# Attention and a gated feed-forward layer on one core: in the first four pairs of heads, the row sums of the softmax move from ScalarE's exponentials to matmuls with ones

## The chip, the cores and the metric

One core of one Trainium2 chip. The metric is the time of one execution in device microseconds; a kernel is run several times and the median is given. All data is float32 in memory. Times inside the program come from one profiled execution.

## What is computed

```python
scores = q @ k.T / sqrt(64)                 # 8 batches, 8 heads, 576 positions, 64 columns
scores = where(row // 64 >= col // 64, scores, -1e9)
attn = exp(scores - max(scores, axis=-1))
attn = attn / (sum(attn, axis=-1) + 1e-9)
x = (attn @ v) as [4608, 512]
h = x @ w_in                                # 512 -> 2048
out = (h / (1 + exp(-1.702 * h))) @ w_out   # 2048 -> 512
```

## The kernel before, in words

**Pairs of heads.** Two heads share the 128 partitions of q and k, so there are 32 pairs (n from 0 to 31), four to a batch. The 576 query rows of a head are cut into five chunks: chunk 0 has 64 rows, chunks 1 to 4 have 128. With the block mask, chunk i sees 64*(2i+1) columns: 64, 192, 320, 448 and 576.

**A pair's way.** `prep` turns q and k with two VectorE transposes (L297), so that their columns lie on the partitions. `score` multiplies them into PSUM banks; chunk 4 is written in two parts, 256 and 320 columns. `weigh` reads a bank on VectorE (L351: add the mask, scale by -0.125, and keep each row's minimum, which is the maximum with its sign turned) and writes the distances to the tile `turned`; then ScalarE takes the exponential in place with the minimum as bias and sums the row in the same instruction (L358). `normalise` adds 1e-9 to the sum and takes the reciprocal on VectorE (L368, L371) and multiplies the chunk by it on GpSimd (L376). `flip` (used for pairs 0 to 7) turns the chunk on TensorE by matmuls with the identity (L102) into a bank, up to four 128x128 squares in each, and ScalarE copies that bank to the second half of `turned` (L411, L424). `av` multiplies the turned weights with v into two banks, o (512 query columns, chunks 1 to 4) and o0 (64, chunk 0), 30 matmuls for a pair; ScalarE copies both to `xr` (L450, L451), the input of the second stage. An fp32 matmul appears as two records in the profile. Later pairs (8 to 31) turn their weights on VectorE and by DMA instead.

**The second stage.** `moe` walks over tiles of 384 of the 4608 rows. `split` cuts a tile of `xr` into a high and a low part in float32r (ScalarE L498, VectorE L82). For each of 16 units of 128 hidden columns there are 12 matmuls into one bank `hp`, a tanh on ScalarE (L562), the gate on VectorE (L563), a cast and a subtraction that split the result (L571, L82), and nine matmuls into the three `acc` banks. The first tile needs all heads of its rows, so pairs 0 to 3. The weights arrive as words of 64 bits and are turned into float32 and split, piece after piece (32 pieces): ScalarE starts a piece (L219), VectorE merges in three steps (L223, L229, L234), ScalarE casts the high part (L243), GpSimd subtracts the low one (L82). One PSUM bank serves these pieces one at a time.

**Order.** TensorE's instructions stay in program order (`mm` and `tr` say so). For the first four pairs it is: scores of chunks 1 and 0 of pair n, turning of chunks 2 and 3 of pair n-1, scores of chunks 2 and 3, turning of chunk 4 of pair n-1, scores of chunk 4, products of pair n-1 with v, turning of chunks 0 and 1 of pair n. On the other engines a scheduler fixes the order when the program is built; each engine then works through its queue in that order, and an instruction that waits holds up all that stands behind it. The PSUM banks of the attention are handed out in a ring of seven by `bank()` until the second stage begins; a bank is used again once its last reader is done. The distances have one buffer for each chunk, shared by all early pairs, and so have the turned weights.

Of the kernel before, what the change touches and what calls it, by code (L numbers as in the profile page):

```python
# [10 lines left out]
F32 = mybir.dt.float32  # L11
F32R = mybir.dt.float32r
U32 = mybir.dt.uint32
AF = mybir.ActivationFunctionType
ALU = mybir.AluOpType
# [14 lines left out]
)  # L30

START = "1+0 - B 2/3 L C - V - 4 - a - - -"
HANDOVER = "B C - 3+0/2+1 - - V - - - 4 - - L - -"
# [7 lines left out]
def attention_moe_kernel(  # L41
# [9 lines left out]
    nc = tc.nc  # L51
    B, H, S, D = q.shape
    DM, DF = w_in.shape
    P = 128
    BLK = 64
# [8 lines left out]
    HP = H // 2  # L64
    NCH = 5

    sp = ctx.enter_context(tc.tile_pool(name="sp", bufs=1))
# [6 lines left out]
    def early(n):  # L74

        return n < 2 * HP

    def phase(n):
        return 0 if n < HP else 1 if n < 2 * HP else 2
# [9 lines left out]
    def bank():  # L89
        tags = ["w0", "w1", "w2"]  # L90
        if not turns["experts"]:
            tags += ["acc0", "acc1", "acc2", "h"]
        elif turns["n"] > 2 * HP:
            tags.append("w3")
        turns["bank"] += 1
        return ps.tile([P, 512], F32, tag=tags[turns["bank"] % len(tags)], name="bank")

    def mm(**kw):
        return tc.keep_in_program_order(nc.tensor.matmul(**kw))  # L99
# [32 lines left out]
    vp = sp.tile([P, 2, NCH, D], F32, name="vp")  # L132
    nc.gpsimd.memset(vp[BLK:P, :, NCH - 1, :], 0.0)
    vx = {}

    def values(n):

        if n not in (1, 3):
            return vp
        if n not in vx:  # L140
            vx[n] = room("xl", [P, 2, NCH, D], F32, "vx")
            nc.gpsimd.memset(vx[n][BLK:P, :, NCH - 1, :], 0.0)
        return vx[n]
# [140 lines left out]
    def load_v(n):  # L284
        to = values(n)
        for hd, b, h in heads(n):
            nc.sync.dma_start(
                out=to[:, hd, 0:QC], in_=v[b, h, 0 : QC * P].rearrange("(c p) d -> p c d", p=P)
            )
            nc.sync.dma_start(out=to[0:BLK, hd, QC], in_=v[b, h, QC * P : S])  # L290
# [49 lines left out]
    def weigh(n, i, hd, lo, hi, s, e):  # L340
        mx, sm = stats[n]
        a, z = qrange(i)
        m = z - a
        w = width(i)
        if early(n):
            e = es[i]
        elif e is None:
            e = d2.tile([P, 2, w], F32, tag=f"e{i % 2}", name="e", bufs=1)
        last = i > 0 and hi == w
        mk = mask[0:m, MW - (hi - lo) : MW] if last else mask[0:m, 0 : hi - lo]  # L350
        nc.vector.tensor_tensor_reduce(  # L351
            out=e[0:m, hd, lo:hi], in0=s, in1=mk,
            op0=ALU.add, op1=ALU.min, scale=-0.125,
            scalar=3e38 if lo == 0 else mx[0:m, NCH, hd : hd + 1],
            accum_out=mx[0:m, i, hd : hd + 1] if hi == w else mx[0:m, NCH, hd : hd + 1],
        )
        if hi == w:
            nc.scalar.activation(  # L358
                out=e[0:m, hd], in_=e[0:m, hd], func=AF.Exp, scale=-1.0,
                bias=mx[0:m, i, hd : hd + 1], accum_out=sm[0:m, i, hd : hd + 1],  # L360
            )
        return e

    def normalise(n, i, e):
        _, sm = stats[n]
        m = BLK if i == 0 else P
        c = sm[0:m, i]
        nc.vector.tensor_scalar(  # L368
            out=c, in0=c, scalar1=1e-9, scalar2=2.0, op0=ALU.add, op1=ALU.mult
        )  # L370
        nc.vector.reciprocal(out=c, in_=c)  # L371
        on = SCALE_ON[phase(n)][i]
        for hd in range(2):
            x, sc = e[0:m, hd], c[:, hd : hd + 1]
            if on == "P":
                nc.gpsimd.tensor_tensor(out=x, in0=x, in1=sc.to_broadcast([m, width(i)]), op=ALU.mult)  # L376
            elif on == "D":
                nc.vector.tensor_scalar(out=x, in0=x, scalar1=sc, scalar2=None, op0=ALU.mult)  # L378
            else:
                nc.scalar.activation(out=x, in_=x, func=AF.Copy, scale=sc)  # L380
# [19 lines left out]

    def flip(n, chunks):

        for i in chunks:
            todo = [(j, hd) for j in range(i) for hd in range(2)]
            for x in range(0, len(todo), 4):
                part = todo[x : x + 4]
                bk = bank()
                for y, (j, hd) in enumerate(part):
                    tr(out=bk[:, y * P : (y + 1) * P], in_=es[i][:, hd, j * P : (j + 1) * P], identity=ident)
                s0 = SLOT[i] + part[0][0]  # L410
                nc.scalar.copy(  # L411
                    out=pw[:, :, s0 : s0 + len(part) // 2].rearrange("p b s h c -> p (s h) b c"),
                    in_=bk[:, 0 : len(part) * P].rearrange("p (x b c) -> p x b c", b=4, c=32),
                )

        bk = bank()
        todo = [(i, hd) for i in chunks for hd in range(2)]
        for y, (i, hd) in enumerate(todo):
            tr(out=bk[0:BLK, y * P : (y + 1) * P], in_=es[i][:, hd, i * P : width(i)], identity=ident)
        src = bk[0:BLK, 0 : len(todo) * P].rearrange("p (x b c) -> p x b c", b=4, c=32)  # L420
        for part in ([0], [1]) if 0 in chunks else (chunks,):
            i, x, a = part[0], 2 * chunks.index(part[0]), 2 if part[0] else 0
            s0 = 9 + max(i, 1)
            nc.scalar.copy(  # L424
                out=pw[0:BLK, a : a + 2, s0 : s0 + len(part)].rearrange("p b s h c -> p (s h) b c"),
                in_=src[:, x : x + 2 * len(part), a : a + 2],
            )

    def av(n):

        b, h = divmod(n, HP)
        before_av(n)
        o, o0 = bank(), bank()

        todo = []
        for i in range(1, NCH):
            c = (i - 1) * P
            todo += [(o, c, P, j, pw[:, :, SLOT[i] + j]) for j in range(i)]
            todo.append((o, c + BLK, BLK, i, pw[:, 2:4, 9 + i]))
        last = len(todo) - 1  # L440
        todo.append((o0, 0, BLK, 0, pw[:, 0:2, 10]))

        for x, (bk, c, nn, j, w) in enumerate(todo):
            for hd in range(2):
                mm(
                    out=bk[hd * D : hd * D + D, c : c + nn].rearrange("d (a c) -> d a c", c=32),
                    lhsT=values(n)[:, hd, j], rhs=w[:, :, hd], start=x in (0, last + 1), stop=x >= last,
                )
        c0 = (b % 2) * S
        nc.scalar.copy(out=xr[:, h, c0 : c0 + BLK], in_=o0[:, 0:BLK])  # L450
        nc.scalar.copy(out=xr[:, h, c0 + BLK : c0 + S], in_=o)  # L451
        m = follower(n)
        if m is not None:
            load_v(m)

    def follower(n):

        m = {0: 2, 1: 3, 2: 4, 3: None}.get(n, n + 1)
        return None if m is None or m >= NPAIR else m
# [205 lines left out]
```

## Time and profile before

| what | value |
|---|---|
| median of 3 runs | 1122.48 us (1120.67 to 1125.02) |
| the profiled execution | 1120.49 us, span 1118.6 us, mean TensorE clock 0.992 |
| TensorE busy | 1076.4 us, 96% of the span |
| VectorE, ScalarE, GpSimd busy | 583.0, 498.6, 406.7 us |
| first matmul of the second stage | 76.91 us |

The page has the span in 40 slices of 28 us; a digit is the busy share of a slice in tenths. A row of a timeline gives the start, the duration, the engine, the line, the operation, what it writes and reads, and in brackets how long the engine stood idle before it and what ended that. A group's row ends with its busy time, the mean of one in ns, and the idle time ahead of it. The engines are PE (TensorE), DVE (VectorE), ACT (ScalarE), POOL (GpSimd).

### The profile page before, as it was taken

What the parts mean: (1) busy time and instruction counts of PE and PEld (TensorE: products, weight loads), DVE (VectorE), ACT (ScalarE), POOL (GpSimd) and SP (SyncE); (2) the same over time, 40 slices, a digit from 0 to 9 for tenths busy, and PEclk for the clock granted to TensorE, in tenths of its full rate; (3) what the DMA queues carried; (4) which work ended last, traced back from release to release, by engine and by line L of the source; (5) the groups of instructions that cost most, each with busy time, mean ns of one, the idle gap of its engine ahead of it and who ended that gap; (6) DMA issues with size and microseconds to landing.
All of it is one profiled execution on the core that took longest, in us unless ns stands there. A gap on an engine that the chain in (4) does not pass through costs nothing. (4 is left out here: it accounts for less than half of the span.)

```text
span 1118.6 us, 19977 instructions
## 1 busy us (share of the span) xinstructions
PE 1076.4 (96%) x6960; PEld 908.7 (81%) x6960; DVE 583.0 (52%) x1856; ACT 498.6 (45%) x1321; POOL 406.7 (36%) x509
## 2 busy tenths in 40 slices
PE   5969998999999999999999999999999999999998
PEld 3757776788888888888888888888888888899997
DVE  6776885545545555654555655645545654211210
ACT  5866776434534433534443543444434444322322
POOL 4665664333333332333333333333333233122222
PEclk9979999999999999999999999999999999999999
DMA  8734532332444432343443333344342332200000
GB/s 171 205 89 153 150 73 62 84 79 57 105 86 86 103 80 64 64 98 78 98 101 74 75 93 65 70 108 85 81 107 63 71 85 58 54 29 1 29 1 29
DMA packets 219365, 91.25 MB, mean 82 GB/s; under 512 B 197760, under 2 KB 197760, under 8 KB 219264
## 3 DMA queue, kind: packets, MB, share of 16 engines
q1 hardware_dynamic: 214528, 89.38, 34.0%
q10 hardware_dynamic: 4736, 0.59, 0.3%
q8 instruction: 55, 0.90, 0.3%
q14 instruction: 46, 0.38, 0.1%
HBM read 45.09 MB, written 9.44 MB: 49 GB/s over the span
## 5 line engine op out<-in xcount | busy, mean ns | idle before, releaser
L82 POOL TENSOR_TENSOR gl<-g,gh 128x384 fp32r<-128x384 f32 x192 | 194.7, 1014 | 551.5 <-ACT gh L571 449.1
L99 PE MATMUL hp<-xh,wih 128*128 128x384 f32 x768 | 264.7, 345 | 7.9 <-DVE g L563 6.9
L563 DVE SCALAR_TENSOR_TENSOR g<-g,hp 128x384 f32<-128x384 f32 x192 | 105.9, 552 | 319.1 <-ACT g L562 317.8
L99 PE MATMUL hp<-xh,wil 128*128 128x384 f32 x768 | 258.4, 336 | 0.1
L562 ACT ACTIVATE g<-hp 128x384 f32<-128x384 f32 x192 | 94.1, 490 | 359.8 <-PE hp L99 354.8
L99 PE MATMUL hp<-xl,wih 128*128 128x384 f32 x768 | 253.9, 338 | 0.4 <-DVE xl L82 0.4
L99 PE MATMUL acc<-woh,gh 128*128 128x512 f32 x576 | 233.9, 406 | 0.0
L99 PE MATMUL acc<-wol,gh 128*128 128x512 f32 x576 | 226.9, 394 | 0.0
L99 PEld LDWEIGHTS hp<-xh,wih 128*128 128x128 f32 x768 | 144.2, 188 | 34.1 <-DVE g L563 23.1
L99 PE MATMUL acc<-woh,gl 128*128 128x512 f32 x576 | 167.9, 393 | 0.3 <-POOL gl L82 0.3
L571 ACT CAST gh<-g 128x384 fp32r<-128x384 f32 x192 | 98.4, 513 | 156.5 <-DVE g L563 156.4
L99 PEld LDWEIGHTS hp<-xh,wil 128*128 128x128 f32 x768 | 144.3, 188 | 6.5 <-POOL wil L82 0.7
L358 ACT ACTIVATE e<-e,mx 64x64 f32<-64x64 f32 (+4 forms) x240 | 132.3, 552 | 37.6 <-DVE mx L351 37.6
L376 POOL TENSOR_TENSOR e<-e,sm 64x64 f32<-64x64 f32 (+1 forms) x192 | 113.6, 612 | 95.0 <-DVE sm L371 46.5
L99 PEld LDWEIGHTS hp<-xl,wih 128*128 128x128 f32 x768 | 143.6, 188 | 1.3 <-DVE xl L82 1.3
L99 PE MATMUL bank<-qk 64*128 64x320 f32 (+4 forms) x768 | 122.5, 428 | 14.5 <-DVE qk L297 11.1
L99 PEld LDWEIGHTS acc<-woh,gh 128*128 128x128 f32 x576 | 107.9, 187 | 34.2 <-issue 10.5
L99 PEld LDWEIGHTS acc<-woh,gl 128*128 128x128 f32 x576 | 107.8, 188 | 25.9 <-POOL gl L82 1.2
L99 PEld LDWEIGHTS acc<-wol,gh 128*128 128x128 f32 x576 | 108.3, 188 | 16.7 <-POOL wol L82 0.3
L351 DVE CUSTOM_DVE_ANT_0 e<-bank,mask 64x64 f32<-64x64 f32 (+4 forms) x240 | 89.7, 417 | 56.9 <-PE bank L99 52.8
L385 DVE STREAM_TRANSPOSE turned<-e 128x384 f32<-128x384 f32 (+1 forms) x192 | 92.3, 499 | 48.8 <-POOL e L376 48.3
L99 PEld LDWEIGHTS bank<-qk 64*128 64x128 f32 x768 | 69.6, 193 | 54.2 <-issue 25.4
(50 smaller groups left out, 956.0 us busy)
## 6 DMA issues: line engine op xcount, KB each, us to landing
turned<-turned SPq DMA_DIRECT2D x192, 80.0 KB, 2.1
turned<-turned SPq DMA_DIRECT2D x96, 112.0 KB, 2.2
raw<-in_q_dram SPq DMA_DIRECT2D x128, 72.0 KB, 2.4
out_dram<-osb SPq DMA_DIRECT2D x36, 256.0 KB, 2.2
raw<-in_k_dram SPq DMA_DIRECT2D x120, 72.0 KB, 2.6
turned<-turned SPq DMA_DIRECT2D x96, 88.0 KB, 2.1
words<-in_moe_w_in_dram SPq DMA_DIRECT2D x16, 512.0 KB, 6.3
vp<-in_v_dram SPq DMA_DIRECT2D x60, 128.0 KB, 2.4
```

The costliest lines, as they stand in the source:

```text
L82: eng.tensor_tensor(out=out, in0=in0, in1=in1, op=ALU.subtract)
L99: return tc.keep_in_program_order(nc.tensor.matmul(**kw))
L351: nc.vector.tensor_tensor_reduce(out=e[0:m, hd, lo:hi], in0=s, in1=mk, op0=ALU.add, op1=ALU.min, scale=-0.125, scalar=3e38 if lo == 0 else ...
L358: nc.scalar.activation(out=e[0:m, hd], in_=e[0:m, hd], func=AF.Exp, scale=-1.0, bias=mx[0:m, i, hd : hd + 1], accum_out=sm[0:m, i, hd : hd ...
L376: nc.gpsimd.tensor_tensor(out=x, in0=x, in1=sc.to_broadcast([m, width(i)]), op=ALU.mult)
L385: nc.vector.transpose(out=tw[:, :, SLOT[i] : SLOT[i] + i, hd].rearrange("p b j c -> p j b c"), in_=e[:, hd, 0 : i * P],)
L562: nc.scalar.activation(out=g, in_=hp[:, 0:tt], func=AF.Tanh, scale=1.702)
L563: nc.vector.scalar_tensor_tensor(out=g, in0=g, scalar=1.0, in1=hp[:, 0:tt], op0=ALU.add, op1=ALU.mult)
L571: nc.scalar.copy(out=gh, in_=g)
```

## The change

For pairs 0 to 3 the rows are no longer divided by their sums before they are turned. `weigh` now subtracts the row's minimum from the distances on GpSimd, without an exponential; `normalise` does nothing. `flip` turns the distances on TensorE, and ScalarE takes the exponential where it copied a bank before. `av` takes a third bank and multiplies the turned weights with a tile of ones, in 28 matmuls for chunks 1 to 4 and two for chunk 0, which leaves the sum of each row in all 64 partitions of its head; then come the 30 products with v. VectorE adds 1e-9 and multiplies by 2, takes the reciprocal, and multiplies the output bank by it into `xr`: three operations on 128x512 and three on 128x64, where ScalarE had two copies. The constant `ones` is set once by GpSimd.

```diff
+    def raw_turned(n):
+        return n < HP
...
+    ones = sp.tile([P, D], F32, name="ones")
+    nc.gpsimd.memset(ones, 1.0)
...
-        if hi == w:
+        if hi == w and raw_turned(n):
+            nc.gpsimd.tensor_tensor(
+                out=e[0:m, hd], in0=e[0:m, hd], in1=mx[0:m, i, hd : hd + 1].to_broadcast([m, w]), op=ALU.subtract
+            )
+        elif hi == w:
             nc.scalar.activation(
                 out=e[0:m, hd], in_=e[0:m, hd], func=AF.Exp, scale=-1.0,
...
     def normalise(n, i, e):
+        if raw_turned(n):
+            return
...
+        def move(out, in_):
+            if raw_turned(n):
+                nc.scalar.activation(out=out, in_=in_, func=AF.Exp, scale=-1.0)
+            else:
+                nc.scalar.copy(out=out, in_=in_)
...
+        c0 = (b % 2) * S
+        if raw_turned(n):
+            o1 = bank()
+            todo0 = [(o0, BLK, BLK, 0, pw[:, 0:2, 10])]
+            sums = [(o1, *x[1:]) for x in todo]
+
+            for some, base in ((sums, ones), (todo0, ones), (todo, None)):
+                for x, (bk, c, nn, j, w) in enumerate(some):
+                    for hd in range(2):
+                        mm(
+                            out=bk[hd * D : hd * D + D, c : c + nn].rearrange("d (a c) -> d a c", c=32),
+                            lhsT=values(n)[:, hd, j] if base is None else base, rhs=w[:, :, hd],
+                            start=x == 0, stop=x == len(some) - 1,
+                        )
+            for hd in range(2):
+                mm(
+                    out=o0[hd * D : hd * D + D, 0:BLK].rearrange("d (a c) -> d a c", c=32),
+                    lhsT=values(n)[:, hd, 0], rhs=pw[:, 0:2, 10, hd], start=True, stop=True,
+                )
+            for a, c, r in ((o, BLK, o1[:, 0:512]), (o0, 0, o0[:, BLK : 2 * BLK])):
+                w = r.shape[1]
+                to = xr[:, h, c0 + c : c0 + c + w]
+                nc.vector.tensor_scalar(out=to, in0=r, scalar1=1e-9, scalar2=2.0, op0=ALU.add, op1=ALU.mult)
+                nc.vector.reciprocal(out=to, in_=to)
+                nc.vector.tensor_tensor(out=to, in0=a[:, 0:w], in1=to, op=ALU.mult)
+            m = follower(n)
+            if m is not None:
+                load_v(m)
+            return
```

In `flip` the two calls of `nc.scalar.copy` become calls of `move`. TensorE's order is the same but for the 30 new matmuls in each of the four pairs.

VectorE's queue between the last scores of pair 2 and the transposes that make ready pair 3 (`qk`), before:

```order
L351 ISA turned_75,mx_433<-bank_546,mask_69,mx_433 128x320
L351 ISA mx_433 128x1
L297 STREAM_TRANSPOSE qk_512<-raw_172 128x576
L368 TENSOR_SCALAR sm_434<-sm_434 128x2
L371 RECIPROCAL sm_434<-sm_434 128x2
L297 STREAM_TRANSPOSE qk_512<-raw_172 128x576
```

and the same place with the change (bank_541 and bank_542 hold pair 1's output, bank_543 its sums):

```order
L358 ISA turned_77,mx_430<-bank_527,mask_69,mx_430 128x320
L358 ISA mx_430 128x1
L304 STREAM_TRANSPOSE qk_493<-raw_158 128x576
L483 TENSOR_SCALAR xr_72<-bank_543 128x512
L484 RECIPROCAL xr_72<-xr_72 128x512
L483 TENSOR_SCALAR xr_72<-bank_542 128x64
L485 TENSOR_TENSOR xr_72<-bank_541,xr_72 128x512
L304 STREAM_TRANSPOSE qk_493<-raw_158 128x576
L484 RECIPROCAL xr_72<-xr_72 128x64
L485 TENSOR_TENSOR xr_72<-bank_542,xr_72 128x64
```

Four of the six new operations stand ahead of the second transpose.

The output of pair 2 before, on ScalarE's queue (bank_762 and bank_763 are its banks; L243 and L219 belong to the weights' pieces):

```order
L243 CAST woh_410<-wm_369 128x512
L219 ACTIVATE wm_416<-words_285 128x512
L243 CAST woh_410<-wm_430 128x512
L219 ACTIVATE wm_460<-words_414 128x512
L451 COPY xr_72<-bank_762 128x512
L450 COPY xr_72<-bank_763 128x64
L411 COPY turned_75<-bank_804 128x2x4x32
L498 CAST xh_977<-xr_72 128x384
```

and with the change, on VectorE's queue (bank_754 and bank_755 hold the output, bank_756 the sums; L230, L236 and L241 are the three merging steps, L358 on bank_849 are pair 4's first scores):

```order
L483 TENSOR_SCALAR xr_72<-bank_756 128x512
L484 RECIPROCAL xr_72<-xr_72 128x512
L304 STREAM_TRANSPOSE qk_702<-raw_286 128x576
L230 TENSOR_SCALAR wm_413<-wm_413 128x512
L236 SCALAR_TENSOR_TENSOR wm_413<-words_259,wm_413 128x512
L241 SCALAR_TENSOR_TENSOR wm_427<-words_259,wm_413 128x512
L230 TENSOR_SCALAR wm_449<-wm_449 128x512
L236 SCALAR_TENSOR_TENSOR wm_449<-words_411,wm_449 128x512
L485 TENSOR_TENSOR xr_72<-bank_754,xr_72 128x512
L241 SCALAR_TENSOR_TENSOR wm_490<-words_411,wm_449 128x512
L483 TENSOR_SCALAR xr_72<-bank_755 128x64
```

The multiplication that empties the output bank stands behind the transpose and five merging steps of two pieces.

The output of pair 3 with the change, again on VectorE (bank_966 and bank_967 hold it, bank_968 the sums; L87 makes the low part of the second stage's first tile, qk_929 is for pair 5):

```order
L483 TENSOR_SCALAR xr_72<-bank_968 128x512
L241 SCALAR_TENSOR_TENSOR wm_678<-words_498,wm_653 128x512
L484 RECIPROCAL xr_72<-xr_72 128x512
L87 TENSOR_TENSOR xl_1040<-xr_72,xh_1039 128x384 x3
L230 TENSOR_SCALAR wm_700<-wm_700 128x512
L304 STREAM_TRANSPOSE qk_929<-raw_705 128x576
L236 SCALAR_TENSOR_TENSOR wm_700<-words_651,wm_700 128x512
L485 TENSOR_TENSOR xr_72<-bank_966,xr_72 128x512
L241 SCALAR_TENSOR_TENSOR wm_731<-words_651,wm_700 128x512
L483 TENSOR_SCALAR xr_72<-bank_967 128x64
L484 RECIPROCAL xr_72<-xr_72 128x64
L485 TENSOR_TENSOR xr_72<-bank_967,xr_72 128x64
```

where before the two copies stood on ScalarE right behind pair 3's last copies out of the turned banks:

```order
L411 COPY turned_75<-bank_920 128x4x4x32
L424 COPY turned_75<-bank_926 64x2x2x32
L451 COPY xr_72<-bank_939 128x512
L450 COPY xr_72<-bank_940 128x64
L498 CAST xh_977<-xr_72 128x384
L243 CAST wih_643<-wm_674 128x512
```

The output's last step moved from ScalarE, where nothing stood between the products and the cast, to VectorE behind other work.

More of the change, by code (lines that the diff above doesn't have):

```diff
@@ L410, in flip @@
                 s0 = SLOT[i] + part[0][0]
-                nc.scalar.copy(
+                move(
                     out=pw[:, :, s0 : s0 + len(part) // 2].rearrange("p b s h c -> p (s h) b c"),
@@ L423, in flip @@
             s0 = 9 + max(i, 1)
-            nc.scalar.copy(
+            move(
                 out=pw[0:BLK, a : a + 2, s0 : s0 + len(part)].rearrange("p b s h c -> p (s h) b c"),
@@ L448, in av @@
                 )
-        c0 = (b % 2) * S
         nc.scalar.copy(out=xr[:, h, c0 : c0 + BLK], in_=o0[:, 0:BLK])
```

## The prediction

> **What bounds the kernel now.** I read the page's slices first, then the waits of TensorE in the first 77 us, then the timelines of TensorE, ScalarE and VectorE there, and last VectorE's groups by form. The page's slices (28 us each), busy tenths of TensorE and its granted clock:
>
> ```profile
> PE   5969998999999999999999999999999999999998
> PEclk9979999999999999999999999999999999999999
> ```
>
> From the fourth slice on TensorE is full, so the span is a start plus a stretch that TensorE sets. The change touches only the first four pairs, which lie in the start; what counts is when the second unit of the experts' first layer begins (81.60 in a row below), since TensorE hardly waits behind it. The waits of TensorE from 0 to 77 us (total, times, longest):
>
> ```profile
> PE bank L99 <- DVE qk L297: 11.1, 4, 7.2
> PE bank L102 <- ACT xr L450: 3.1, 1, 3.1
> PE bank L99 <- ACT turned L411: 2.3, 2, 1.6
> PE bank L102 <- POOL turned L376: 2.2, 1, 2.2
> ```
>
> Of the first row 7.2 us is the first load; the other 3.9 are waits for q and k of the next pair to be turned. TensorE's timeline of the start (start, us, engine, line, operation, count in matmul records, two for one matmul in fp32):
>
> ```profile
> 7.23 5.71 PE L99 MATMUL bank<-qk 64*128 64x192 f32 x24 [7.23 <-DVE qk L297]
> ...
> 32.15 0.76 PE L99 MATMUL bank<-qk 64*128 64x192 f32 x8 [0.58 <-DVE qk L297]
> 32.84 1.75 PE L102 MATMUL bank<-ident,turned 128*128 128x128 f32 x14
> 34.52 1.98 PE L99 MATMUL bank<-qk 64*128 64x320 f32 x8
> 36.42 1.31 PE L102 MATMUL bank<-ident,turned 128*128 128x128 f32 x10
> 37.67 1.24 PE L99 MATMUL bank<-qk 64*128 64x256 f32 x8
> 38.84 2.99 PE L99 MATMUL bank<-turned,vx 128*64 128x128 f32 x60
> 41.75 0.88 PE L102 MATMUL bank<-ident,turned 128*128 128x128 f32 x6
> 43.42 0.76 PE L99 MATMUL bank<-qk 64*128 64x192 f32 x8 [0.79 <-DVE qk L297]
> ...
> 52.38 2.98 PE L99 MATMUL bank<-turned,vp 128*64 128x128 f32 x60
> ...
> 58.69 0.76 PE L99 MATMUL bank<-qk 64*128 64x192 f32 x8 [2.52 <-DVE qk L297]
> ...
> 63.16 2.37 PE L102 MATMUL bank<-ident,turned 128*128 128x128 f32 x10 [3.12 <-ACT xr L450]
> 66.33 3.88 PE L99 MATMUL bank<-qk 64*128 64x320 f32 x8 [0.80 <-ACT turned L424]
> 70.14 2.39 PE L102 MATMUL bank<-ident,turned 128*128 128x128 f32 x10
> 72.46 3.73 PE L99 MATMUL bank<-turned,vx 128*64 128x128 f32 x60
> ...
> 81.60 0.44 PE L99 MATMUL hp<-xh,wih 128*128 128x384 f32 x1 [1.79 <-DVE g L563]
> ```
>
> Rows 32.15 to 41.75 are one pair on a TensorE that hardly waits: 0.76 + 1.75 + 1.98 + 1.31 + 1.24 = 7.04 us from its first scores to its last, 2.99 for the products with v, 0.88 to turn the next two chunks. From 63.16 on the same work takes about twice as long, 4.8 us more over four rows: the clock has dropped. Why TensorE waits at 63.16 stands on ScalarE's queue (casts and first steps of the weights' conversion, then the copies that empty the bank):
>
> ```profile
> 61.35 0.62 ACT L243 CAST woh<-wm 128x512 fp32r<-128x512 f32 x1 [2.29 <-DVE wm L234]
> 61.88 0.62 ACT L219 ACTIVATE wm<-words 128x512 f32<-128x512 f32 x1
> 62.44 0.58 ACT L451 COPY xr<-bank 128x512 f32<-128x512 f32 x1
> 62.91 0.21 ACT L450 COPY xr<-bank 128x64 f32<-128x64 f32 x1
> ```
>
> The products ended at 52.38 + 2.98 = 55.36; the copy that frees their bank stood behind two casts that wait for VectorE. So an instruction that empties a bank is priced by what is queued ahead of it.
>
> **The change, part by part.** VectorE's groups by form (count, busy, mean ns):
>
> ```profile
> L297 DVE STREAM_TRANSPOSE qk<-raw 128x576 f32<-128x576 f32 x64 | 46.7, 758 | 5.8 <-DMA raw<-in_q_dram 5.7
> L82 DVE TENSOR_TENSOR xl<-xr,xh 128x384 fp32r<-128x384 f32 x48 | 27.1, 605 | 22.5 <-ACT xh L498 22.0 <-PE bank L99 0.5
> L223 DVE TENSOR_SCALAR wm<-wm 128x512 uint32<-128x512 uint32 x32 | 22.3, 696 | 15.9 <-ACT wm L219 15.9
> L229 DVE SCALAR_TENSOR_TENSOR wm<-words,wm 128x512 uint32<-128x512 uint32 x28 | 19.3, 688 | 0.3
> L234 DVE SCALAR_TENSOR_TENSOR wm<-words,wm 128x512 uint32<-128x512 uint32 x28 | 19.0, 680 | 0.7
> L371 DVE RECIPROCAL sm<-sm 128x2 f32<-128x2 f32 x128 | 21.0, 164 | 3.7
> L351 DVE CUSTOM_DVE_ANT_0 turned<-bank,mask 128x448 f32<-128x448 f32 x16 | 9.7, 613 | 4.9 <-PE bank L99 4.9
> L351 DVE CUSTOM_DVE_ANT_0 turned<-bank,mask,mx 128x320 f32<-128x320 f32 x16 | 8.4, 537 | 0.1
> L351 DVE CUSTOM_DVE_ANT_0 turned<-bank,mask 128x320 f32<-128x320 f32 x16 | 7.5, 484 | 0.6 <-PE bank L99 0.3
> L351 DVE CUSTOM_DVE_ANT_0 turned<-bank,mask 128x256 f32<-128x256 f32 x16 | 6.5, 414 | 0.9 <-PE bank L99 0.9
> L351 DVE CUSTOM_DVE_ANT_0 turned<-bank,mask 128x192 f32<-128x192 f32 x16 | 5.1, 341 | 0.0
> L351 DVE CUSTOM_DVE_ANT_0 turned<-bank,mask 64x64 f32<-64x64 f32 x16 | 3.2, 210 | 3.8 <-PE bank L99 3.7
> ```
>
> *TensorE* gets 30 matmuls more for a pair, of the shapes of row 38.84: 2.99 us, 12.0 for four pairs, in its fixed order and so on the path. *ScalarE* loses ten exponentials, their sums and two copies for a pair, and its nine copies out of the turned banks become exponentials. I take those at the copies' price; they add nothing to the end while ScalarE has the freed time. *GpSimd* keeps ten full-size operations for a pair, a subtraction where a multiplication was, of the same sizes: nothing, but they wait for VectorE's minima alone. That takes away the 2.2 us wait for GpSimd.
>
> *VectorE* loses ten small operations and gets six with a pair's output: add and multiply on 128x512 (0.70, by row L223), a reciprocal, a multiplication with the output bank (0.69, by row L229), and the same on 64 columns (0.2, by the 64x64 row, except the reciprocal). A wide reciprocal is not in the trace. VectorE's timeline has a narrow one:
>
> ```profile
> 52.53 0.15 DVE L371 RECIPROCAL sm<-sm 128x2 f32<-128x2 f32 x1
> 52.60 0.40 DVE L351 CUSTOM_DVE_ANT_0 turned<-bank,mask 128x256 f32<-128x256 f32 x1
> ```
>
> The next instruction starts 0.07 us behind it, so an element costs at most 35 ns: 512 cost at most 18 us. At least they cost what other arithmetic of that shape does, 0.70. One row has the shape, the other the operation, and neither is near, so I take their geometric middle, 3.5 us, an estimate; for 64 columns 0.65 between 0.2 and 2.2. The Trainium skill, "VectorE: DVE Perf Modes", section "Walkthrough: the 8-slice pipeline in each mode", has the reciprocal as an iterated divide with a repeat count of 8; were that eight passes for each element, at 1.0 ns for a column (the 448 against the 320 row) it would be 4.1 us, an estimate, and the sum below some 3 us longer; no run here shows it.
>
> What lies behind these six on VectorE is what costs: the second transpose for the next pair (all of the next scores wait for it), and the release of the banks. By the queue orders shown above:
>
> 1. *To the products of pair 0.* TensorE's first scores end at 12.94. VectorE's queue then holds two transposes (1.52), the last four scores of pair 0 (1.90), eight of pair 1 (3.30) and four of six merging steps (2.76) before the bank for pair 1's last scores is free: from 12.35 to 21.9, so they end at 22.3, the last matmul being 0.4. Sums and products, 2 x 2.98: 28.2.
> 2. *Scores of pair 2.* VectorE from 21.9: 1.37 of merging, 1.90 of scores, 0.76 of transpose, 25.9; then 0.70 + 3.5 + 0.2 + 0.69 + 0.65 + 0.2 and the second transpose, 0.76: 32.6. Before 32.15: the gain is gone.
> 3. *Scores of pair 3.* 32.6 + 7.04 + 2.99 puts the sums at 42.6; 0.70 + 3.5 + 0.2 + 0.69 + 0.76: 48.5. Before 43.42, +5.1.
> 4. *Scores of pair 4.* From 48.5 VectorE has 0.85 left of pair 1, 0.42 of scores, then two pieces' merging among pair 3's scores: 2.07 + 0.68 + 0.97 + 0.61 + 0.70 + 0.61, 55.4. There the last scores of pair 3 can start; the sums of pair 2 are done at 58.9. VectorE goes on: 0.69 + 0.41 + 0.68 + 0.41 + 1.07, then 1.38 + 0.76 + 0.68 of piece 4 and a transpose, 61.5; 0.70 + 3.5 + 0.76: 66.5. Before 58.69, +7.8.
> 5. *The banks of pair 2's output.* VectorE then merges piece 5 (2.07), waits for ScalarE's cast and start of piece 6 (1.24), does two steps of it (1.38), and only then multiplies the output (0.69); a merge (0.68) and 1.5 on 64 columns follow. The banks are free at 74.1; before at 63.16, +10.9.
> 6. *To the experts.* At the low clock the rows from 63.16 to 72.46 take 9.3 again: 83.4. Sums 3.73: 87.1. VectorE: 0.70 + 0.68 + 3.5, three subtractions for the experts' first tile (1.8), 0.70 + 0.76 + 0.69, the multiplication, 0.69 + 0.68, 64 columns 1.05: 98.4. ScalarE's cast of that column block is over at 99; the seventh matmul of the first unit waits for it, where before it came right behind the products. From that matmul to 81.60 it was 3.7 us: 102.6. That is 21.0 us later; I take off 0.6 for one cast that stood before the first tanh and by the order now stands ahead of this wait, and call it 20.
>
> The profiled execution took 1120.49 us (span 1118.6), 2.0 below the median of three, 1122.48. 1120.5 + 20 = 1140.5 against the profile; as the median I say 1141.
>
> **Rivals.** *The reciprocal runs at the plain rate*, 0.7 and 0.2. Steps 2, 3 and 4 then end at 29.4, 43.8 and 58.5: pairs cost what they did, with 12 us of matmuls paid by the waits that go. Step 5 gives 65.6 and step 6 an end 9 us later: 1130. For it speaks that the narrow reciprocal is no longer than its neighbours, against it only how little a row of two elements can say.
>
> *No change.* The plain rate, and the scheduler's queue behind pair 2 is harmless since the merges ahead of the multiplication run while VectorE would idle, so that TensorE keeps its clock: 1130 less 4.8 and less part of the 3 us of ScalarE's wait: 1123. Against it speaks that each merge waits for ScalarE's cast of the piece before, on one bank.
>
> *Faster*, one mechanism: the idle time of TensorE pays for the sums. Place: its stalls from 12.9 to 77 us. Price: the waits above come to 11.5 us without the first load, the low clock costs 4.8; with the 12.0 us of new matmuls that is 4 us less, and up to 8 less if the smaller waits go too: 1116 to 1112. It decides if VectorE's output work of pairs 0 to 2 is over within 1 us of the products, so that no transpose and no bank waits for it; then a wide reciprocal may not cost over about 1 us, and merging may not stand ahead of pair 2's multiplication. In the queue's order it does stand there.
>
> That the work does not move is no rival: the order shows the new operations.
>
> **Numbers.** My case 0.56, the plain rate 0.26, no change 0.11, faster 0.07. A measurement tells 0.5%, 5.6 us, from no change. My case is slower; of the plain rate I count 0.21 as slower and 0.05 as within. So slower 0.77, same 0.16, faster 0.07. The range reaches from the lower part of the plain rate, 1124, to a reciprocal over 4 us with two or three more us of low clock, 1150.
>
> **What would show it.** Right: a wide RECIPROCAL of some us on VectorE; scores of pair 3 near 48 us and of pair 4 near 66, waiting for qk; the transposes of chunks 2 and 3 of pair 3 waiting for VectorE until over 70; the second unit of the experts near 102; unchanged group means behind it. Wrong: a wide reciprocal under 1 us; the start not longer than 82 us; exponentials out of the banks clearly above the copies' 0.58; a shift that is not in the first 110 us.

## The result, and the profile after

The changed kernel takes 1131.68 us (four runs, 1130.99 to 1133.36) where the kernel before, run beside it, takes 1123.75: a ratio of 1.0075, with a 95% interval from 1.006 to 1.0091. So it is slower by 7.9 us; forecast was 1141, in a range from 1124 to 1150. Its profiled execution took 1131.48 us (span 1129.7), 11.0 more than the profiled execution of before.

The page's slices show where: the second to the fourth read 867, where before they read 969, and behind them TensorE is as full as before.

```profile
PE   7867999999999999999999999999999999999998
PEclk9988999999999999999999999999999999999999
```

To say how late each stretch is, I compare the start of the same instruction in both traces: ScalarE's cast that begins to split the result of a unit of the experts' first layer (192 of them). Its first one, its 13th, its 16th and its last, before and then after (start, duration):

```profile
81.58 0.51 ACT L571 CAST gh<-g 128x384 fp32r<-128x384 f32 x1
166.30 0.50 ACT L571 CAST gh<-g 128x384 fp32r<-128x384 f32 x1
197.41 0.51 ACT L571 CAST gh<-g 128x384 fp32r<-128x384 f32 x1 [1.71 <-DVE g L563]
1111.61 0.51 ACT L571 CAST gh<-g 128x384 fp32r<-128x384 f32 x1 [0.62 <-DVE g L563]
```

```profile
95.22 0.50 ACT L619 CAST gh<-g 128x384 fp32r<-128x384 f32 x1
180.34 0.53 ACT L619 CAST gh<-g 128x384 fp32r<-128x384 f32 x1
207.45 0.51 ACT L619 CAST gh<-g 128x384 fp32r<-128x384 f32 x1 [1.71 <-DVE g L611]
1122.63 0.51 ACT L619 CAST gh<-g 128x384 fp32r<-128x384 f32 x1 [0.62 <-DVE g L611]
```

The shift is +13.6 us at the first unit, +14.0 at the 13th, +10.0 at the 16th, +11.0 at the last. All of the loss is made in the first 95 us; then 4 us are given back between 166 and 208 us, and 1 us is lost again behind that.

The three largest waits of TensorE from 0 to 100 us after (total, times, longest):

```profile
PE bank L104 <- DVE qk L304: 15.0, 5, 7.4
PE hp L104 <- ACT xh L546: 6.5, 1, 6.5
PE bank L107 <- DVE xr L485: 5.2, 2, 4.7
```

They are those for q and k (15.0, before 11.1), for the multiplication that empties an output bank (5.2; before 3.1, for a copy), and one of 6.5 that was 0.7 before, for the cast of pair 3's output. The waits for GpSimd have gone, as forecast. TensorE's timeline:

```profile
21.53 2.99 PE L104 MATMUL bank<-turned,ones 128*64 128x128 f32 x60
24.35 2.94 PE L104 MATMUL bank<-turned,vp 128*64 128x128 f32 x60
...
30.76 0.76 PE L104 MATMUL bank<-qk 64*128 64x192 f32 x8 [2.67 <-DVE qk L304]
...
45.50 0.76 PE L104 MATMUL bank<-qk 64*128 64x192 f32 x8 [1.90 <-DVE qk L304]
...
63.17 0.76 PE L104 MATMUL bank<-qk 64*128 64x192 f32 x8 [2.80 <-DVE qk L304]
...
68.60 1.09 PE L107 MATMUL bank<-ident,turned 128*128 128x128 f32 x4 [4.67 <-DVE xr L485]
70.19 2.37 PE L107 MATMUL bank<-ident,turned 128*128 128x128 f32 x10 [0.50 <-DVE xr L485]
72.49 2.34 PE L104 MATMUL bank<-qk 64*128 64x320 f32 x8
74.76 1.31 PE L107 MATMUL bank<-ident,turned 128*128 128x128 f32 x10
76.00 2.62 PE L104 MATMUL bank<-turned,ones 128*64 128x128 f32 x44
...
91.21 0.69 PE L104 MATMUL hp<-xh,wih 128*128 128x384 f32 x1 [6.51 <-ACT xh L546]
...
94.67 0.69 PE L104 MATMUL hp<-xh,wih 128*128 128x384 f32 x1 [1.17 <-DVE g L611]
```

Each wait of the start stands where the queue orders put it. Two things more. From 72.49 on the clock comes back (the same 64x320 scores took 3.88 before, 2.34 now; the next ten records 2.39 before, 1.31 now). And it had dropped once already behind the scores of pair 3: the 14 records at 46.19 took 2.72 us, where before they took 1.75, and from 46 to 50 us the granted clock was 0.60. VectorE's groups have the price that no trace of before could give (count, busy, mean ns):

```profile
L384 DVE RECIPROCAL sm<-sm 128x2 f32<-128x2 f32 x112 | 18.4, 164 | 3.5
L484 DVE RECIPROCAL xr<-xr 128x512 f32<-128x512 f32 x4 | 13.4, 3351 | 0.1
L484 DVE RECIPROCAL xr<-xr 128x64 f32<-128x64 f32 x4 | 2.1, 536 | 0.0
L485 DVE TENSOR_TENSOR xr<-bank,xr 128x512 f32<-128x512 f32 x4 | 2.7, 685 | 0.0
```

The wide reciprocal takes 3351 ns for 512 columns, against the 3.5 us that I took, and 536 for 64, against 0.65. ScalarE's groups, exponentials out of the banks (L419) beside the copies that later pairs still make (L421):

```profile
L419 ACT ACTIVATE turned<-bank 128x512 f32<-128x512 f32 x16 | 8.8, 591 | 7.8 <-PE bank L107 7.8
L421 ACT COPY turned<-bank 128x512 f32<-128x512 f32 x16 | 8.6, 583 | 1.9 <-PE bank L107 1.9
```

591 against 583 ns is a difference of nothing, as assumed.

### The profile page after: what moved, and what is told of

It reads as the page before. It is cut to its first block, busy times and chain, and to the rows that moved or that the text cites. A ratio compares the mean times of both kernels' runs of the same rounds, so it can differ in the third digit from the quotient of the medians.

```text
span 1129.7 us, 20353 instructions
## 1 busy us (share of the span) xinstructions
PE 1085.3 (96%) x7200; PEld 921.6 (82%) x7200; DVE 594.6 (53%) x1840; ACT 474.8 (42%) x1233; POOL 406.1 (36%) x510
## 5 line engine op out<-in xcount | busy, mean ns | idle before, releaser
L87 POOL TENSOR_TENSOR gl<-g,gh 128x384 fp32r<-128x384 f32 x192 | 194.5, 1013 | 548.1 <-ACT gh L619 441.7
L104 PE MATMUL bank<-qk 64*128 64x320 f32 (+4 forms) x768 | 119.8, 426 | 15.8 <-DVE qk L304 15.0
L358 DVE CUSTOM_DVE_ANT_0 e<-bank,mask 64x64 f32<-64x64 f32 (+4 forms) x240 | 89.8, 417 | 57.0 <-PE bank L104 52.9
```

The costliest lines, as they stand in the source:

```text
L87: eng.tensor_tensor(out=out, in0=in0, in1=in1, op=ALU.subtract)
L358: nc.vector.tensor_tensor_reduce(out=e[0:m, hd, lo:hi], in0=s, in1=mk, op0=ALU.add, op1=ALU.min, scale=-0.125, scalar=3e38 if lo == 0 else ...
```

## The experiments

Theory A, mine: the wide reciprocals on VectorE and the place of the output's work in VectorE's queue cost the time. The rivals: the matmuls with ones on TensorE cost it (B); or the merging steps that stand in VectorE's queue ahead of the outputs do (C). The exponentials on ScalarE got no kernel of their own; the 591 against 583 ns above speaks against them.

### Without the reciprocals, and without the sums

The first kernel is the changed one without its eight wide reciprocals (the output isn't divided):

```diff
                 nc.vector.tensor_scalar(out=to, in0=r, scalar1=1e-9, scalar2=2.0, op0=ALU.add, op1=ALU.mult)
-                nc.vector.reciprocal(out=to, in_=to)
                 nc.vector.tensor_tensor(out=to, in0=a[:, 0:w], in1=to, op=ALU.mult)
```

> Leaves out the division by the row sums in pairs 0 to 3: the eight reciprocals (3.35 and 0.54 us each) are gone, the sums are still made, read and multiplied in. Theory A (the reciprocals stand ahead of the transposes for the next pair, of the freeing of the banks and of the experts' first tile): the waits for qk fall from 2.7, 1.9 and 2.8 us to under 1 each, the wait before the experts' first tile from 6.5 to under 3, and the time from 1131.7 to 1119 to 1123. Rival B (the 12 us of new matmuls are the price, the waits only move): 1129 to 1132. Rival C (the merging steps ahead of pair 2's multiplication are the price): the waits for the output banks, 4.7 us, stay, and the time falls by 3 to 5 us, to about 1127.

Measured: 1122.56 us, ratio to before 0.9993 (0.9984 to 1.0002), in A's range. The reciprocals are worth 9.1 us, more than the change loses. Its waits from 0 to 100 us:

```profile
PE bank L104 <- DVE qk L304: 10.0, 4, 7.2
PE bank L107 <- DVE xr L484: 4.7, 1, 4.7
PE hp L104 <- ACT xh L545: 4.1, 1, 4.1
```

The waits for q and k behind the first load fall from 7.6 to 2.8 us. The wait for the cast falls by 2.4, to 4.1, not under 3 as A had it. The bank of pair 2 is waited for as long as in the changed kernel (4.7), as C had it, though it is free 7.3 us earlier (61.30 against 68.60): the merging that stands ahead of its multiplication is still there.

This kernel does not show that the rest of the change is free. Its first unit is still 3.9 us later than before (cast at 85.45 against 81.58), the 13th 7.1 us, and only then, by the 16th, do 4.4 us come back, through a new order on GpSimd that has nothing to do with the division (see "Where 3 us come back"). Where the 3.9 us are made stands on TensorE's timeline:

```profile
76.25 0.44 PE L104 MATMUL hp<-xh,wih 128*128 128x384 f32 x1
...
81.64 0.44 PE L104 MATMUL hp<-xh,wih 128*128 128x384 f32 x1 [4.08 <-ACT xh L545]
```

The second stage's first matmul comes 0.7 us earlier than before (76.25 against 76.91), with all the sums in the way; then TensorE waits 4.08 us for the cast of pair 3's output, whose multiplication stands on VectorE behind low parts, merging steps and a transpose. So in the start the division is the larger part of the price, and the output's place in VectorE's queue the rest.

The second kernel keeps the reciprocals and leaves out 26 of the 30 matmuls with ones of a pair (the sums are unfinished):

```diff
-            for some, base in ((sums, ones), (todo0, ones), (todo, None)):
+            for hd in range(2):
+                mm(
+                    out=o1[hd * D : hd * D + D, 0:512].rearrange("d (b s c) -> d b s c", b=4, c=32),
+                    lhsT=ones, rhs=pw[:, :, 6:10, hd], start=True, stop=True,
+                )
+            for some, base in ((todo0, ones), (todo, None)):
```

> Leaves out 26 of the 30 matmuls with ones of each of the four pairs: one matmul over 512 columns for each head stands for the sums of chunks 1 to 4, so that the numbers are not the rows' sums, and VectorE does all it did. Theory A and rival B both have TensorE's sums on the path, since the reciprocal can only start behind them: about 2.5 us less for a pair, 1121 to 1124. If VectorE's queue alone sets the start (rival C), the sums are hidden: 1128 or more.

Measured: 1138.5 us, ratio 1.0134 (1.0115 to 1.0153). With some 7.2 us of TensorE's work less (a pair's sums take 1.19 us here instead of 2.99), it is 6.8 us slower than the changed kernel. The "1128 or more" for a start that VectorE's queue alone sets does hold it, but nothing here expected a loss. Its timeline at pair 2:

```profile
30.15 1.33 PE L104 MATMUL bank<-qk 64*128 64x192 f32 x8 [4.03 <-DVE qk L304]
31.41 3.25 PE L107 MATMUL bank<-ident,turned 128*128 128x128 f32 x14
```

The scores of pair 2 start only 0.6 us earlier than with all the sums (30.15 against 30.76), because VectorE sets that time: the waits for q and k have grown from 15.0 to 20.0 us. So the sums' matmuls lay in time in which TensorE would have waited. Besides, TensorE has stood idle 4.03 us instead of 2.67, and its clock has halved: the scores take 1.33 us instead of 0.76, and the next 14 records, 1.75 in the changed kernel, 3.25.

One such place could be chance, but the mean granted clock of whole executions goes the same way in three pairs of kernels, without an overlap. It is 0.982 to 0.985 here and 0.986 to 0.988 in the changed kernel; 0.988 to 0.991 in the third kernel below and 0.992 to 0.994 without the reciprocals alone; 0.986 to 0.992 in the kernel before and 0.994 to 0.995 with the sums added to it (further below). Each time the kernel with more matmuls with ones has the higher clock.

The third kernel does both (no division, unfinished sums), to see whether the sums cost once VectorE no longer sets the pace.

> Leaves out of the changed kernel both the eight wide reciprocals (no division) and 26 of the 30 matmuls with ones of each of the first four pairs (sums unfinished). Alone, the first takes 9 us off, the second adds 7. Theory A: VectorE's queue sets the pace of the start as long as the reciprocals are in it, so the sums' matmuls only fill time in which TensorE would wait; with the reciprocals gone TensorE sets the pace again and 26 x 0.1 x 4 = 10 us of matmuls come off, less what is lost to waits for q and k and to the lower clock behind them: 1113 to 1119, waits for qk behind the first load under 6 us. Rival B: even without the reciprocals VectorE (transposes, merging, scores) and the low clock set the pace of the start, and the sums' matmuls fill idle time there too: 1121 to 1125, qk waits behind the first load over 8 us.

Measured: 1122.82 us, ratio 1.0 (0.9989 to 1.0011), the same as without the reciprocals alone. The time is B's. The waits for q and k behind the first load, though, are 4.4 us, as A had them and not over 8; the time went elsewhere. (By the rows 7.2 us of matmuls came off, not the 10 that I expected.) Its waits from 0 to 100 us:

```profile
PE bank L104 <- DVE qk L304: 11.4, 5, 7.0
PE bank L107 <- DVE xr L489: 5.3, 1, 5.3
PE hp L104 <- ACT xh L550: 4.2, 1, 4.2
PE bank L104 <- ACT turned L419: 4.0, 1, 4.0
```

TensorE comes to pair 4 at 52.29, where without the reciprocals alone it comes at 55.80, and then waits for VectorE's multiplication, ScalarE's exponentials and the cast. The first unit is only 1.3 us earlier than without the reciprocals alone, and of the two kernels it has the lower mean clock. So with the other engines' queues as they are, 26 of the 30 matmuls of a pair cost about nothing at the end.

### The sums alone, in the kernel before

The kernel before with 30 matmuls with ones for each of the first four pairs, behind the products with v, whose result nobody reads:

```diff
+        if n < HP:
+            o1 = bank()
+            for some in ([(o1, *x[1:]) for x in todo], [(o0, BLK, BLK, 0, pw[:, 0:2, 10])]):
+                for x, (bk, c, nn, j, w) in enumerate(some):
+                    for hd in range(2):
+                        mm(
+                            out=bk[hd * D : hd * D + D, c : c + nn].rearrange("d (a c) -> d a c", c=32),
+                            lhsT=ones, rhs=w[:, :, hd], start=x == 0, stop=x == len(some) - 1,
+                        )
```

> The kernel before, with the 30 matmuls with ones for each of the first four pairs added and nobody reading the sums. Rival B: 12 us more than before, about 1135. Theory A: the waits of the start that VectorE and ScalarE set (0.6, 0.8, 2.5 and 3.1 us) take up part of them: 5 to 9 us more, 1129 to 1132.

Measured: 1125.75 us, ratio 1.0013 (1.0002 to 1.0023). Both expectations were too high for the end. By the trace the first unit is 8.4 us later, of 12.0 us that the matmuls take, which is in A's 5 to 9; the 16th is 5.8 later and the last one 5.4: by the 16th, 2.6 us have come back. It is one more kernel in which some 3 us come back between 160 and 210 us.

### Where 3 us come back

In that stretch the kernel before waits 3.1 us for GpSimd, in two waits (`PE bank L102 <- POOL turned L376`), the changed one not at all. Before, GpSimd's timeline at pair 7's last chunk, whose two heads are multiplied one after the other:

```profile
184.77 1.15 POOL L376 TENSOR_TENSOR turned<-turned,sm 128x576 f32<-128x576 f32 x1
185.88 1.26 POOL L82 TENSOR_TENSOR wol<-wm,woh 128x512 fp32r<-128x512 f32 x1
187.09 1.15 POOL L376 TENSOR_TENSOR turned<-turned,sm 128x576 f32<-128x576 f32 x1
```

A piece of the weights stands between the two, and TensorE's matmuls for that chunk wait. In the changed kernel the scheduler has put the two together:

```profile
195.54 2.25 POOL L389 TENSOR_TENSOR turned<-turned,sm 128x576 f32<-128x576 f32 x2 [4.78 <-ACT g L610]
```

The change touches nothing there. To test it, the kernel before with a priority for that one step:

```diff
-                normalise(n, i, e[i])
+                with tc.high_priority(offset=300 if n == 2 * HP - 1 and i == NCH - 1 else 0):
+                    normalise(n, i, e[i])
```

> The kernel before, with one change to GpSimd's queue: the two multiplications of pair 7's chunk 4 stand together, ahead of a weights' piece and a subtraction that stood before or between them. TensorE waits 3.1 us for the second of them in the kernel before, and not in the changed kernel. Theory A with a gift behind the start (the change's new order lets these 3 us go, which has nothing to do with sums): 2 to 3 us less than before, 1120.5 to 1121.5. If the 3 us come back elsewhere: no change, 1123.6.

Measured: 1119.18 us where before takes 1122.98, ratio 0.9962 (0.9947 to 0.9977), somewhat more than the 2 to 3 us expected. Its trace has no wait for GpSimd from 160 to 220 us, and is equal to that of before up to the 13th unit within 1.1 us. So this order is worth 3 to 4 us, and the changed kernel has it by chance, through the scheduler. This kernel is faster than both.

The 7.9 us of the change are therefore a loss of some 11.7 less a gift of 3.8 through GpSimd's order (an estimate: no run has the changed kernel without the gift). By the same estimate the kernel without reciprocals would, without it, be some 2.8 us slower than before (3.8 - 1.0).

### The change for some pairs

For pair 0 alone, and for pairs 0 to 2 (with 3 in place of 1), the other pairs staying as they were in the kernel before:

```diff
     def raw_turned(n):
-        return n < HP
+        return n < 1
```

> The change for pair 0 alone. Theory A: the wait for GpSimd (2.2 us) and the low clock behind it go, 3 us of matmuls come, and one reciprocal stands ahead of pair 2's transpose: from 1 us less to 2 us more than before, 1122 to 1126. Rival B: 3 us more, 1126.5.

> The change for pairs 0 to 2 alone; pair 3 as before. Theory A: the wait of 6.5 us before the experts' first tile goes, with the low clock behind it (1.5 us) and 3 us of matmuls, while pair 3 gets back its waits of old: 8 to 10 us less, 1122 to 1124. Rival B: 3 us less, 1128 to 1129.

Measured: pair 0 alone 1125.62 us, ratio 1.0024 (1.0013 to 1.0034), which is in A's range and 0.9 us from B's time and so decides nothing. Pairs 0 to 2: 1130.49 (1128.92 to 1134.72), ratio 1.0068 (1.0042 to 1.0095), not 1122 to 1124 as I expected if the long tail behind pair 3 were most of the loss, and above B's 1128 to 1129 too. In its trace, of an execution slower than its median (1134.72, at a granted clock of 0.985), the tail has gone (the second unit starts at 90.95, 3.7 us earlier than in the changed kernel), but the 3.1 us of waits for GpSimd near 200 us are there again, and the clock drops in another place:

```profile
57.37 5.44 PE L104 MATMUL bank<-turned,ones 128*64 128x128 f32 x60 [2.82 <-ACT turned L419]
```

Sums that take 2.98 at the full clock took 5.44. So this kernel does not settle how much pair 3's tail costs at the end; a gain in the start was met by two losses that the whole change does not have.

### Moving the waits

If the second transpose of a pair stood ahead of the reciprocal, nothing would wait for q and k. The queue that loads k decides that order through the scheduler; the line was changed so that pairs 2 to 4 have k through ScalarE's queue too:

```diff
-            queue = nc.scalar if n < 2 and x else nc.sync
+            queue = nc.scalar if n < 5 and x else nc.sync
```

> The changed kernel, with the loads of k for pairs 2 to 4 issued from ScalarE's queue, so that the scheduler puts both transposes for the next pair ahead of the reciprocals. Theory A (the reciprocals ahead of the transposes are the price): the waits for qk, 7.4 us in pairs 2 to 4, fall under 2, and the time from 1131.7 to 1122 to 1127. Rival B (the sums' matmuls): 1130 or more. Rival C (the merging steps in the way): the merging moves ahead of the outputs as well, so the waits for banks grow, 1128 or more.

Measured: 1135.46 us, ratio 1.0108 (1.0093 to 1.0123), slower than the changed kernel: A's 1122 to 1127 is out. B's "1130 or more" holds, and so does C's "1128 or more"; the waits, from 0 to 100 us, are what C had:

```profile
PE bank L107 <- DVE xr L485: 9.7, 5, 3.9
PE bank L104 <- DVE qk L304: 7.1, 1, 7.1
PE hp L104 <- ACT xh L546: 4.9, 1, 4.9
```

The wait for q and k is only the first load's, as meant. The waits for the multiplication that frees the banks take its place (9.7 against 5.2), and one of 4.9 for the cast is left. VectorE's timeline shows what moved:

```profile
27.48 1.43 DVE L304 STREAM_TRANSPOSE qk<-raw 128x576 f32<-128x576 f32 x2
28.83 0.67 DVE L230 TENSOR_SCALAR wm<-wm 128x512 uint32<-128x512 uint32 x1
...
35.11 3.35 DVE L484 RECIPROCAL xr<-xr 128x512 f32<-128x512 f32 x1
```

Both transposes of pair 2 run before pair 0's output, but two pieces' merging (six steps, the first at 28.83) went ahead too. So the reciprocals' place ahead of the transposes is not by itself the price: with the transposes first, the banks wait instead.

The other way round, the output's three operations get priority, which puts pair 3's multiplication ahead of the second stage's low parts, a transpose and three merging steps:

```diff
-            for a, c, r in ((o, BLK, o1[:, 0:512]), (o0, 0, o0[:, BLK : 2 * BLK])):
+            with tc.high_priority(offset=300):
+                for a, c, r in ((o, BLK, o1[:, 0:512]), (o0, 0, o0[:, BLK : 2 * BLK])):
```

> The changed kernel with priority for the three VectorE operations on an output, which alters the queue mostly behind pair 3's products: the multiplication and the 64 columns then stand ahead of three low parts of the second stage, a transpose and three merging steps. Theory A (what stands in the queue ahead of the multiplication costs, step 6): the wait of TensorE for the cast of pair 3's output, 6.5 us in the changed kernel, falls to 2.5 to 4 us, the second unit of the experts comes 3 us earlier, and with it the end: 1127.5 to 1129.5. Rival B: what is put behind takes the place (low parts and merging late, the gate or the weights' pieces waited for): the second unit at the same time within 1 us, 1131 to 1133.

Measured: 1132.16 us, ratio 1.008 (1.0062 to 1.0099), no faster than the changed kernel. Its timeline:

```profile
30.35 1.18 PE L104 MATMUL bank<-qk 64*128 64x192 f32 x8 [2.67 <-DVE qk L304]
31.46 2.94 PE L107 MATMUL bank<-ident,turned 128*128 128x128 f32 x14
...
64.95 1.33 PE L104 MATMUL bank<-qk 64*128 64x192 f32 x8 [2.19 <-DVE qk L304]
...
90.56 0.44 PE L104 MATMUL hp<-xh,wih 128*128 128x384 f32 x1 [3.24 <-ACT xh L547]
...
93.88 0.69 PE L104 MATMUL hp<-xh,wih 128*128 128x384 f32 x1 [1.88 <-DVE g L612]
```

The wait for the cast falls from 6.51 to 3.24, as theory A said: the order behind pair 3 makes about half of that wait. But the scores of pairs 3 and 4 come 1.6 and 1.8 us later (47.11 and 64.95). Of that, 1.6 us is a lower clock from pair 2's scores on: the rows at 30.35 and 31.46 take 1.18 and 2.94 us where the changed kernel has 0.76 and 1.75, behind the same wait of 2.67. Some 0.4 more goes to the one small reciprocal of pair 1 that priority moved ahead of a transpose (a wait of 2.32 against 1.90); pair 2's scores themselves start 0.4 earlier. More waits for exponentials follow, the second stage's first matmul comes at 86.00 instead of 83.37, and the second unit is only 0.8 us earlier. So the time is B's, with A's mechanism inside it.

### The kernel before, once more

> The kernel before once more, for a second profile: its profiled execution of 1120.5 us lies 3 us under the median of its runs. If the start differs from run to run, the first unit of the experts lies 2 to 4 us later than in the first profile (81.6 us); if something later does, the first unit lies at 81 to 82 and the difference comes behind it.

Measured: 1120.12 us, and every unit within 0.4 us of the first profile. Both profiled executions of before lie some 3 us under the median of its timed runs. The mean granted clock of an execution goes with it. The 19 runs of before beside the second group of kernels, by clock:

| mean granted clock | runs | us |
|---|---|---|
| 0.986 | 2 | 1125.17 to 1125.38 |
| 0.988 | 3 | 1123.83 to 1123.97 |
| 0.989 | 10 | 1123.09 to 1124.47 |
| 0.991 | 3 | 1122.07 to 1123.58 |
| 0.992 | 1 | 1120.74 |

Both profiled executions had 0.992, which only 4 of the 47 runs of before listed with these experiments had. So the 11.0 us between the profiles is more than the change costs between ordinary runs; 7.9 is the figure.

## Why the prediction was right in sign and too high

The steps, forecast against measured (us):

| step | forecast | measured | off |
|---|---|---|---|
| 1, products of pair 0 end | 28.2 | 27.3 | -0.9 |
| 2, scores of pair 2 | 32.6 | 30.76 | -1.8 |
| 3, scores of pair 3 | 48.5 | 45.50 | -3.0 |
| 4, scores of pair 4 | 66.5 | 63.17 | -3.3 |
| 5, banks of pair 2 free | 74.1 | 70.19 | -3.9 |
| 6, sums of pair 3 start | 83.4 | 76.00 | -7.4 |
| 6, second unit | 102.6 | 94.67 | -7.9 |
| end, against the profile | 1140.5 | 1131.48 | -9.0 |

Of the 9.0 us, 3.9 come from steps 1 to 5, 3.5 from the rows that open step 6, 0.5 from the rest of it, and 1.1 from what lies behind it.

**Right.** The mechanism: q and k late behind a reciprocal of 3.35 us; the bank of pair 2 behind merging; the cast of pair 3's output last. Leaving the reciprocals out takes 9.1 us off, which shows that they are the larger part of the price; that the time is then that of before is the gift on GpSimd too. The size of the reciprocal was luck: 3.5 was the middle between 0.70 and 18, and neither bound was near.

**Step 6 failed most**, in "at the low clock the rows from 63.16 to 72.46 take 9.3 again". They took 76.00 - 70.19 = 5.8 us: 3.5 too many. The low clock is 2.6 of these (3.88 against 2.34 and 2.39 against 1.31; the first row takes 2.37 in both), and 0.8 is the wait for ScalarE's copy inside them, which the changed kernel does not have there. I carried both over as if they belonged to those rows. The low clock does not: it comes behind idle time of TensorE, in other places in each kernel. After, it lies at 46.19, at 68.60 and again near 95 us; in the kernel without most sums at 30 us; with the change for three pairs at 57. The Trainium skill, "TensorE: Matmul & The Clock Gate", section "Part 1: The HAM clock gate (the "warmup" mystery)", has TensorE's clock halved after an idle window of about 3.4 us. By the same section of the Trainium skill the window runs freely, whatever the kernel does, and so the number of slow matmuls at a kernel's start differs from run to run. The rows agree in the half rate (2.98 against 5.44, 1.75 against 3.25); they do not agree that a wait must be so long, since the clock dropped behind single waits of 1.90, 2.19 and 2.67 us. A window was not measured here.

**Sums of durations run long.** Steps 1 to 5 gather 3.9 us of small excess. I added durations of rows; starts are closer together. In before 7.04 us of rows from 32.15 fill 38.84 - 32.15 = 6.69; after, the reciprocal at 81.80 lasts 3.35 and the next instruction starts at 85.06, 3.26 later:

```profile
81.80 3.35 DVE L484 RECIPROCAL xr<-xr 128x512 f32<-128x512 f32 x1
85.06 1.43 DVE L87 TENSOR_TENSOR xl<-xr,xh 128x384 fp32r<-128x384 f32 x3
```

With 0.35 to a pair on TensorE and 0.08 to each instruction of VectorE, four pairs make several us; how much of the 3.9 that is, I have not separated. (One length was misread by a little: the seventh matmul of the first unit starts at 78.06, so 3.5 us before 81.60 and not 3.7.)

**The assumption that the shift carries to the end** was off by 2.6 us (13.6 at the first unit, 11.0 at the last). "TensorE hardly waits behind it" is right on average, and the scheduler still put GpSimd's queue near 190 us in another order, though the change is not there (shown by the priority in the kernel before). No step had a term for it.

**The median.** The forecast was 18.5 us over the median, the result 7.9. Of the 11.0 us between the profiles 3 are not there between ordinary runs, because the execution of before on which the sum stood had a clock that few of its runs have. No step of the sum holds these 3 us. The 1141 mixed the two as well: it is some 20 us above the profile, and 20 above the median would have been 1142.5.

**The rivals.** The plain rate is out: on 512 columns the reciprocal takes 4.9 times what the multiplication beside it takes (3351 against 685), on 64 columns 2.4 times (536 against 224). Its price of 1130 was too high as well: with the reciprocal left out altogether the time is 1122.6. That is also the 1123 that "no change" had for a cheap reciprocal, but by luck: the merging was not harmless (the bank of pair 2 was waited for 4.7 us), and the gift made up for it. "Faster" named two conditions, a reciprocal under 1 us and no merging ahead of pair 2's multiplication. Neither holds; with the first met alone, and even with few sums, the first unit is no earlier than before (3.9 and 2.6 us later). The second alone was not tried. Each pair's sums I priced at 2.98 us on the path; in the changed kernel leaving most of them out gained nothing, since VectorE sets the pace there, and in the kernel before they cost 8.4 of 12.0 us at the first unit.

## What to carry to other kernels

A division moved behind a product is cheap only if it has few columns: count the reciprocal's columns, not its rows (64x2 took 155 ns, 128x2 164, 128x512 3351), and put it where no transpose and no bank waits behind it on its engine. TensorE's work that lies in its idle time was free here, and taking it out cost, with a lower clock. Never carry a low-clock stretch from one trace to another, and look along the whole trace for orders that a scheduler changed where the code did not: here such an order hid 3 to 4 us of the price.

## What the runs showed of the hardware

- VectorE's reciprocal costs (3351 - 536) / 448 = 6.3 ns a column, where the multiplication from a bank costs (685 - 224) / 448 = 1.0. By that rate two columns would take 536 - 62 x 6.3 = 145 ns, near the 164 of the narrow row: nearly all of the narrow row's time is a fixed part, which is why it said so little of the wide one. The Trainium skill, "VectorE: DVE Perf Modes", section "Walkthrough: the 8-slice pipeline in each mode", has an iterated divide with a repeat count of 8; my estimate from that, 4.1 us, is above the 3.35 measured.
- The length of TensorE's last wait alone does not decide whether its clock drops. Behind the same wait of 2.67 us ahead of pair 2's scores, the next 14 records took 1.75 us in the changed kernel, 2.94 in the one with priority for the outputs and 3.00 in the one with the change for three pairs. What else decides was not tried.
